# Where k^T v and one subtraction stand in the order of a fused attention and feed-forward kernel

## The chip, the cores and the metric

The kernel runs on one core of a Trainium2 chip. The core has a matrix engine (TensorE, PE in the profile), a vector engine (VectorE, DVE), an activation engine (ScalarE, ACT), a general engine (GpSimd, POOL) and DMA queues; each engine works through its own list of instructions in order, and semaphores hold an instruction back until what it needs is there. The metric is the device time of one execution in microseconds (us). The time before is 917.43 us, the median of three runs (916.87 to 917.55).

## What is computed

Two blocks follow each other. The first is an attention without softmax, with a norm over each head's output; the second a feed-forward block with a squared ReLU:

```python
kv = np.einsum('bhsd,bhse->bhde', k, v)          # 8 x 8 heads, 576 x 64 each
out = np.einsum('bhsd,bhde->bhse', q, kv)
rms = np.sqrt(np.mean(out * out, axis=-1, keepdims=True) + 1e-06)
x = out / rms * g_norm                            # laid out as (4608, 512)
h = x @ w_in                                      # (4608, 2048)
g = s * np.maximum(h, 0.0) ** 2 + b
result = g @ w_out                                # (4608, 512)
```

All data is float32.

## The kernel before

**Units.** The 4608 tokens are cut into 36 chunks of 128, and four chunks make a unit, so there are nine units, u = 0 to 8. In each unit the first product (x times w_in), the activation, and the second product (g times w_out) are done for 512 tokens, both with Strassen-like schemes: sums and differences of quarters are made on DVE, seven products are made on PE instead of eight, and their results are put together again while they are read out of PSUM. Units 2 to 8 use the scheme at two levels in many places. Beside this work, the attention of the next unit is prepared, in two pairs of chunks, A and B.

**The order is written by hand.** No planner moves anything. The first product of units 2 to 8 is `mm1_deep`, whose `run` (line 928) lists the steps one by one: `x1`, `x6`, `y7`, `x5`, `y4` are products of full 128 by 128 tiles, `small(...)` are those of the second level with 128 columns, `a22(s)` reads a y bank. Between them stand calls `at(n)`, and what is done at mark n is given by the table `first` in `sides` (line 1658). In the kernel before, for units 3 to 7, the table has the turn of pair A's q at mark 2, A's product at 4, `back` at 5, the square and B's turn at 6, the row sum and, behind it, k^T v at 7, the norm at 8, B's product at 10, and so on.

**The attention steps.** `product` (line 553) multiplies the turned q with the block-diagonal matrix `bd_kv` in small tiles (64 rows by 32 columns), line 561. `kv_product(b)` (line 370) makes k^T v for one batch with 144 matmuls of 64 by 64 tiles (line 382), and four ACT copies (line 398) put the result into `bd_kv[b % 2]`. The batch is given by `kv_due`: 2 to 7 in units 1 to 6. The k and v rows come through the same ring of buffers in SBUF as the weights of the second product; `used(...)` gives ring slots back in order, and the next loads are issued then.

**PSUM.** Four groups of banks: `ps_t` (tag t, two buffers) for the small products of the attention and for k^T v; `sx` for the second level; and in `ps_f` the x banks (two), the y banks (two) and the z bank (one) for the large products. `bank_of(key, tag, bufs)` takes the next bank of a tag. A bank is used again when its last reader is done.

**The second product.** For units 2 to 8 the function `rest` (line 1377) inside `mm2` lists the steps. Names: a group such as 25 stands for the products 2 and 5 of the outer level. `go_25(m)` issues product m of the inner level on PE; `out_25(m)` reads its result on DVE (line 1092, about 0.35 to 0.5 us); `do_25(m)` is both, one after the other; `sums_25(...)` makes the sums on DVE (lines 250 and 253). `s2` and `s4` are four DVE subtractions each, one for every quarter of the hidden dimension, of 128 by 512 elements:

```python
def s4(steps=range(NS)):
    for s in steps:
        sub(ga["a12", s], ga["a12", s], ga["a11", s])
```

The result of s4 is an operand of the group 73. Around it the order is: `do_25(4)`, `do_6(2, 6)`, then all four s4, `go_6(7)`, `do_6(5)`, the sums of 73, `go_73(1)`, and so on to `do_73(2)`, `sums_73((7,))`, `do_73(6)`, `sums_73((3,))`, `go_73(7)`.

Of the kernel before, what the change touches and what calls it, by code (L numbers as in the profile page):

```python
# [9 lines left out]
FP32 = mybir.dt.float32  # L10
# [6 lines left out]
def kernel(  # L17
# [40 lines left out]
    P = 128  # L58
    B, H, S, D = q.shape
# [23 lines left out]
    ps_t = ctx.enter_context(tc.tile_pool(name="ps_t", bufs=2, space=bass.MemoryType.PSUM))  # L83
# [283 lines left out]
        for _ in range(n):  # L367
            matmul(ps[:, 0, :P], ident, ident, True, True)

    def kv_product(b):  # L370


        ps = [ps_t.tile([P, 2, D], FP32, name="kv_ps", tag="t") for _ in range(2)]
        for i in range(2):
            if b == 0:
                warm((18, 7)[i])
            kv = [kv_in.pop((b, 2 * i + l)) for l in range(2)]
            for j in range(R):
                for l in range(2):
                    for r in range(2):  # L380
                        rows = slice(r * HB, r * HB + HB)
                        nc.tensor.matmul(  # L382
                            ps[r][(r ^ l) * HB : (r ^ l) * HB + HB, i, :],
                            lhsT=kv[l][0][rows, j, :],
                            rhs=kv[l][1][rows, j, :],
                            start=(j == 0),
                            stop=(j == R - 1),
                        )
        for r in range(2):
            rs = slice(r * HB, r * HB + HB)  # L390
            for l in range(2):
                cs = slice((r ^ l) * HB, (r ^ l) * HB + HB)
                to = bd_kv[b % 2][rs, l:NP:2, rs].rearrange("p i (c e) -> p i c e", c=KC)
                src = ps[r][cs].rearrange("p i (e c) -> p i c e", c=KC)
                if b == 0 and l == 1:
                    nc.vector.tensor_copy(out=to, in_=src)
                else:
                    nc.scalar.copy(to, src)
# [248 lines left out]
    def bank_of(key, tag, bufs=2):  # L647
        bank[key] = ps_f.tile([P, 2, TB], FP32, name=f"{tag}_ps", tag=tag, bufs=bufs)
        return bank[key]
# [420 lines left out]
    def mm2(u, step=None, side={}):  # L1070
# [133 lines left out]
        def store(name, j, c, cols=slice(0, DM), queues=(nc.gpsimd, nc.gpsimd)):  # L1204
            view = out_9 if c < R else out_18
            w = view.shape[2]
            for s, (b, jj) in enumerate((b, jj + i) for b, jj, n in parts(c) for i in range(n)):
                queues[s % 2].dma_start(  # L1208
                    out=view[b, jj, :, cols], in_=st[name, j][s * w : s * w + w, cols]
                )  # L1210
# [36 lines left out]
# [3 lines that stand above are left out]
# [127 lines left out]
        def rest():  # L1377
            do_1(1)
            step["x3"]()
            step["x3_square"]()  # L1380
            step["y4"]()
            do_1(2)
            step["y4_square"]()
            do_1(6)
            step["x3_s1"]()
            go_1(7)
            do_1(5)
            sums_25((5, 6), 2)
            sums_25((7,), 5)
            at(0)  # L1390
            do_25(1)
            do_1(3)
            sums_25((5, 6), 5)
            do_1(4)
            do_25(2)
            at(1)
            step["x3_s3"]()
            s2((0,))
            do_25(6)
            s2((1,))  # L1400
            sums_25((3,))
            go_25(7)
            s2((2,))
            do_25(5)
            s2((3,))
            sums_6(())
            do_6(1)
            sums_6((5, 6))
            at(2)
            do_25(3)  # L1410
            sums_6((7, 3))
            do_25(4)
            if end:
                for j in range(2):
                    store("o1", j, 4 * u + j, left, queues)
            do_6(2, 6)
            s4((0, 1))
            s4((2, 3))
            go_6(7)
            do_6(5)  # L1420
            sums_73((5, 6), 7)
            sums_73((), 3)
            go_73(1)
            with_5(0, cols[0])
            out_73(1)
            do_6(3)
            with_5(0, cols[1])
            sums_73((5, 6), 3)
            do_6(4)
            with_5(1)  # L1430
            do_73(2)
            sums_73((7,))
            at(3)
            do_73(6)
            sums_73((3,))
            at("sums")
            go_73(7)
            do_73(5)
            sums_4((5, 6))
            do_4(1)  # L1440
            at(4)
            do_73(3)
            with_7(0)
            sums_4((7, 3))
            go_73(4, 7)
            out_73(4, slice(0, 1))
            with_7(1)
            if end:
                for j in range(2):
                    store("o2", j, 4 * u + 2 + j, right, queues)  # L1450
                store("o1", 0, 4 * u, right, queues)
            else:
                store("o1", 0, 4 * u, queues=queues)
            do_4(2, 6)
            go_4(7)
            do_4(5)
            at(5)
            go_73(4, 3)
            out_73(4, slice(1, 2))
            if end:  # L1460
                store("o1", 1, 4 * u + 1, right, queues)
            else:
                store("o1", 1, 4 * u + 1, queues=queues)
            do_4(3)
            at(6)
            if end:
                store("o2", 0, 4 * u + 2, left, queues)
            else:
                store("o2", 0, 4 * u + 2, queues=queues)
            do_4(4)  # L1470
            if end:
                store("o2", 1, 4 * u + 3, left, queues)
            else:
                store("o2", 1, 4 * u + 3, queues=queues)
# [183 lines left out]
    def sides(u, A, B):  # L1658

        first, second = {}, {}
        kv = []
        if u in kv_due:
            kv.append(lambda: kv_product(kv_due[u]))
            kv.append(lambda: used(*((u, "kv", (n, m)) for n in range(NP) for m in range(2))))
        q = {half: [partial(loads, u + 2, half)] for half in range(2)}
        if u == 1:
            for s in range(1, NS):
                first[((0, 1), (0, 3), (1, 1))[s - 1]] = list(sums_w_in(s))  # L1670
            first.update({
                (1, 3): kv,
                (2, 0): [partial(A["turn"], 0), partial(A["turn"], 1)],
                (2, 1): [A["product"]],
                (2, 2): [A["back"]],
                (2, 3): [A["square"]],
                (3, 0): [A["row_sum"]],
                (3, 2): [A["norm"], A["turn_x"]],
                (3, 3): [lambda: [load() for load in load_q(12, rest_on=nc.sync)]],
            })  # L1680
            return first, second
        if u + 1 == U:
            return first, second
        if u == 2:
            first = {
                4: [A["turn"]],
                5: kv,
                8: [A["product"]],
                9: [A["back"], B["turn"]],
                10: [A["square"]],  # L1690
                11: [A["row_sum"]],
                12: [B["product"]],
                13: [A["norm"]],
                14: [A["turn_x"]],
                15: [B["back"], *q[0]],
                18: [B["square"]],
            }
            second = {
                0: [B["row_sum"]], 1: [A["scale"]], 2: [B["norm"]], 3: [B["turn_x"], *q[1]],
                "sums": [B["scale"]],  # L1700
            }
        else:
            first = {
                2: [A["turn"]],
                4: [A["product"]],
                5: [A["back"]],
                6: [A["square"], B["turn"]],
                7: [A["row_sum"], *kv],
                8: [A["norm"]],
                9: [A["turn_x"]],  # L1710
                10: [B["product"], *q[0]],
                11: [B["back"], A["scale"]],
                12: [B["square"]],
                13: [B["row_sum"]],
                14: [B["norm"]],
                15: [B["turn_x"], *q[1]],
            }
            second = {1: [B["scale"]]}
        second[5], second[6] = [[lambda n=n: x_sums(u + 1)[n]()] for n in range(2)]
        return first, second  # L1720

    for u in range(U):
        A, B = pairs_of(u + 1) if u + 1 < U else (None, None)
# [92 lines left out]
```

## Time and profile before

| | |
|---|---|
| time, median of 3 runs | 917.43 us |
| span of the profiled execution | 915.9 us, 19161 instructions |
| PE (matmul) busy | 903.1 us, 99% |
| DVE busy | 695.5 us, 76% |
| ACT busy | 254.3 us, 28% |
| DMA | 180.33 MB, 197 GB/s on average |
| k^T v matmuls (line 382) | 1152, of which 864 from the ring |
| TensorE clock granted | 0.999 |

In the profile every matmul is two instructions on two tracks: PEld for the load of the weights and PE for the product. A float32 product of the program is two such pairs, so a product with eight matmuls in the profile has four in the program. A line such as "0.48 DVE L1092 ... x1 [0.18 <-PE z_ps L91]" reads: a duration of 0.48 us, the engine, the line of the program, the operands, how many in a row, and that the engine stood idle for 0.18 us before it until PE had written z_ps. PE is shown as busy nearly all the time, so what it loses is found in three ways: in its waits, in what the chain that ended last holds apart from PE, and in the lengths of stretches that hold the same work.

### The profile page before, as it was taken

How to read it: one execution, taken by the hardware profiler on the slowest of the kernel's cores; microseconds unless marked ns; L12 is line 12 of the kernel's file. 1: busy time of each engine (PE TensorE's matmuls, PEld its weight loads, DVE VectorE, ACT ScalarE, POOL GpSimd, SP SyncE). 2: the span in 40 equal slices, each digit the busy share in tenths (PEclk: the TensorE clock that was granted, in tenths of full speed). 3: DMA queues.
4: the chain of work that ended last, by engine and by line, in shares of the span. 5: the costliest groups of instructions: out<-in, count | busy, mean ns of one | idle time of the engine just before them, and what ended most of it. 6: DMA issues, size and time to landing. Idle time of an engine off the chain costs nothing.

```text
span 915.9 us, 19161 instructions
## 1 busy us (share of the span) xinstructions
PE 903.1 (99%) x7524; PEld 827.9 (90%) x7524; DVE 695.5 (76%) x1266; ACT 254.3 (28%) x463; POOL 223.5 (24%) x418
## 2 busy tenths in 40 slices
PE   7999999999999999999999999999999999999998
PEld 7888888888889998999899988999899989999997
DVE  2779778688568986888678867886788778874786
ACT  3774122211135014410343015401450035002500
POOL 2000016114622332801283026503340300020000
PEclk9999999999999999999999999999999999999999
DMA  9677937339943994379436945596538811881185
GB/s 267 214 276 271 267 94 230 96 92 385 340 131 90 290 309 138 84 250 307 145 104 196 293 163 162 131 308 222 150 98 284 281 36 53 278 298 49 54 255 183
DMA packets 120137, 180.33 MB, mean 197 GB/s; under 512 B 29168, under 2 KB 46320, under 8 KB 120048
## 3 DMA queue, kind: packets, MB, share of 16 engines
q1 hardware_dynamic: 101552, 153.00, 53.2%
q0 software_dynamic: 15040, 23.88, 8.6%
q10 hardware_dynamic: 3456, 2.23, 1.0%
q8 instruction: 60, 0.98, 0.4%
q14 instruction: 29, 0.24, 0.1%
HBM read 153.36 MB, written 25.69 MB: 195 GB/s over the span
## 4 chain that ended last, share of the span: by engine, by line
PE 86%; DVE 11%; issue 1%; DMA 1%; ACT 0%; SPq 0%; DVEq 0%
PE x_ps L91 43%; PE y_ps L91 26%; PE z_ps L91 7%; PE sx_ps L91 4%; DVE a L253 2%; PE y_ps L561 2%; DVE sub L253 2%; PE kv_ps L382 2%; DMA kv_sb<-in_v_dram 1%; DVE sub L250 1%; DVE o L1092 1%; DVE b_row L250 1%; DVE r L1092 1%; DVE o L250 1%; DVE w_dn L245 0%
## 5 line engine op out<-in xcount | busy, mean ns | idle before, releaser
L1633 POOL DMA_DIRECT2D q_sb<-in_q_dram x256 | 143.7, 569 | 141.5 <-issue 116.4
L1208 POOL DMA_DIRECT2D out_dram<-o x110 | 54.8, 505 | 408.1 <-DVE o L1092 285.0
L91 PE MATMUL x_ps<-w_sb,sub 128*128 128x128 f32 x1176 | 149.4, 276 | 0.1
L91 PEld LDWEIGHTS x_ps<-w_sb,sub 128*128 128x128 f32 x1176 | 139.7, 192 | 1.2 <-DVE r L1092 0.5
L91 PE MATMUL y_ps<-xs,wb 128*128 128x256 f32 x512 | 121.1, 381 | 0.7 <-DVE ss L584 0.7
L91 PE MATMUL x_ps<-xs,ws 128*128 128x256 f32 x512 | 121.3, 380 | 0.0
L91 PEld LDWEIGHTS y_ps<-xs,wb 128*128 128x128 f32 x512 | 94.6, 190 | 14.6 <-issue 2.8
L91 PEld LDWEIGHTS x_ps<-xs,ws 128*128 128x128 f32 x512 | 93.9, 190 | 11.4 <-issue 0.4
L91 PE MATMUL x_ps<-xT,wa 128*128 128x256 f32 x384 | 89.0, 381 | 0.1
L829 ACT COPY a<-x_ps 128x512 f32<-128x512 f32 x28 | 16.4, 586 | 257.8 <-PE x_ps L91 257.8
L91 PEld LDWEIGHTS x_ps<-xT,wa 128*128 128x128 f32 x384 | 71.3, 190 | 10.9 <-issue 1.3
L250 DVE TENSOR_TENSOR r<-sx_ps,a 128x256 f32<-128x256 f32 x63 | 26.7, 423 | 59.0 <-PE sx_ps L91 58.9
L91 PE MATMUL x_ps<-w_sb,a 128*128 128x128 f32 (+1 forms) x432 | 64.9, 298 | 0.0
L91 PE MATMUL y_ps<-w_sb,a 128*128 128x128 f32 (+1 forms) x416 | 62.1, 295 | 0.0
L91 PEld LDWEIGHTS x_ps<-w_sb,a 128*128 128x128 f32 x432 | 59.0, 191 | 3.3 <-issue 0.4
L91 PEld LDWEIGHTS y_ps<-w_sb,a 128*128 128x128 f32 x416 | 56.1, 192 | 2.1
L1092 DVE SCALAR_TENSOR_TENSOR r<-x_ps,s_col,o 128x256 f32<-128x256 f32 (+1 forms) x84 | 34.7, 413 | 29.1 <-PE x_ps L91 27.8
L91 PE MATMUL y_ps<-w_sb,sub 128*128 128x128 f32 x392 | 50.2, 277 | 2.3 <-DVE sub L253 2.3
L91 PEld LDWEIGHTS y_ps<-w_sb,sub 128*128 128x128 f32 x392 | 46.5, 192 | 3.7 <-DVE sub L253 3.7
L250 DVE TENSOR_TENSOR a<-y_ps,r 128x512 f32<-128x512 f32 x36 | 24.8, 688 | 32.3 <-PE y_ps L91 23.8
L253 DVE TENSOR_TENSOR a<-a,a 128x512 f32<-128x512 f32 x72 | 46.8, 685 | 0.4
L91 PE MATMUL z_ps<-w_sb,a 128*128 128x128 f32 (+1 forms) x352 | 46.8, 280 | 0.0
(190 smaller groups left out, 1489.5 us busy)
## 6 DMA issues: line engine op xcount, KB each, us to landing
w_sb<-w SPq DMA_DIRECT2D x385, 256.0 KB, 4.4
w_raw<-in_moe_w_in_dram SPq DMA_DIRECT2D x8, 1024.0 KB, 7.6
w_raw<-in_moe_w_out_dram SPq DMA_DIRECT2D x8, 1024.0 KB, 5.2
w_sb<-w SPq DMA_DIRECT2D x14, 512.0 KB, 10.2
w<-sub POOLq DMA_DIRECT2D x28, 256.0 KB, 6.3
w_sb<-in_k_dram SPq DMA_DIRECT2D x24, 288.0 KB, 4.6
w_sb<-in_v_dram SPq DMA_DIRECT2D x24, 288.0 KB, 4.7
out_dram<-o POOLq DMA_DIRECT2D x92, 64.0 KB, 3.5
```

The lines of the kernel that those rows point to most:

```text
L91: nc.tensor.matmul(o, lhsT=lhsT, rhs=rhs, start=start, stop=stop, skip_group_check=True)
L250: nc.vector.tensor_tensor(out=o, in0=a, in1=b, op=ALU.add)
L253: nc.vector.tensor_tensor(out=o, in0=a, in1=b, op=ALU.subtract)
L382: nc.tensor.matmul(ps[r][(r ^ l) * HB : (r ^ l) * HB + HB, i, :], lhsT=kv[l][0][rows, j, :], rhs=kv[l][1][rows, j, :], start=(j == 0), sto ...
L561: nc.tensor.matmul(ps[l][32 * p : 32 * p + 32, r, lo:hi], lhsT=bd_kv[b % 2][rows, p, at : at + 32], rhs=st["qT"][rows, p, lo:hi], start=Tr ...
L829: nc.scalar.copy(g_tile("a11", s), st["x", s])
L1092: nc.vector.scalar_tensor_tensor(o, ps, s_col, other, ALU.mult, ALU.add)
L1208: queues[s % 2].dma_start(out=view[b, jj, :, cols], in_=st[name, j][s * w : s * w + w, cols])
L1633: load()
```

## The change

Two things are moved; no work is added or left out.

First, in units 3 to 6, k^T v is no longer done at mark 7 behind A's row sum, but at mark 4, right behind A's product. As the two `ps_t` banks are then still full of that product, k^T v takes the z bank and one y bank instead; `kv_product` has a new argument `beside` for this. Units 0 to 2 keep the old banks and places. The purpose is to let the two kinds of small-tile matmuls follow each other, and to have the ACT copies and the ring's slots earlier.

Second, in `rest`, that is in units 2 to 8, the first of the four s4 subtractions is made before `do_6(2, 6)` and not after it.

```diff
-    def kv_product(b):
-
-
-        ps = [ps_t.tile([P, 2, D], FP32, name="kv_ps", tag="t") for _ in range(2)]
+    def kv_product(b, beside=False):
+        if beside:
+            ps = [
+                bank_of("kv", tag, bufs).rearrange("p b (m d) -> p (b m) d", d=D)[:, :2]
+                for tag, bufs in (("z", 1), ("y", 2))
+            ]
+        else:
+            ps = [ps_t.tile([P, 2, D], FP32, name="kv_ps", tag="t") for _ in range(2)]
...
+            s4((0,))
             do_6(2, 6)
-            s4((0, 1))
-            s4((2, 3))
+            s4((1, 2, 3))
             go_6(7)
             do_6(5)
...
-            kv.append(lambda: kv_product(kv_due[u]))
+            kv.append(lambda: kv_product(kv_due[u], u > 2))
...
             first = {
                 2: [A["turn"]],
-                4: [A["product"]],
+                4: [A["product"], *kv],
                 5: [A["back"]],
                 6: [A["square"], B["turn"]],
-                7: [A["row_sum"], *kv],
+                7: [A["row_sum"]],
```

## The prediction

> **What bounds the kernel now.** I read the page first, then the waits of PE, then the chain of waits in order of time, and last the timeline around the two places that the change touches.
>
> ```profile
> PE 903.1 (99%) x7524; PEld 827.9 (90%) x7524; DVE 695.5 (76%) x1266; ACT 254.3 (28%) x463; POOL 223.5 (24%) x418
> ...
> PE 86%; DVE 11%; issue 1%; DMA 1%; ACT 0%; SPq 0%; DVEq 0%
> ```
>
> PE is the bound. The change removes no work, so it can only give back PE's idle time and the time that PE spends changing from one kind of tile to another. But 11% of the chain that ended last is DVE: there are stretches where PE follows DVE closely. The waits of PE show how little is really lost (columns: total us, times, longest):
>
> ```profile
> PE y_ps L91 <- DVE sub L253: 2.3, 7, 0.5
> ...
> PE y_ps L91 <- DVE ss L584: 0.7, 1, 0.7
> ```
>
> The first is one wait in each of the units 2 to 8. The timeline of unit 3 shows where it comes from (start, duration, engine, in brackets the idle time before):
>
> ```profile
> 409.58 0.48 DVE L1092 SCALAR_TENSOR_TENSOR o<-y_ps,s_col,r 128x256 f32<-128x256 f32 x1
> ...
> 410.24 0.35 DVE L1092 SCALAR_TENSOR_TENSOR o<-z_ps,s_col,r 128x128 f32<-128x128 f32 x1 [0.18 <-PE z_ps L91]
> ...
> 411.13 0.35 DVE L1092 SCALAR_TENSOR_TENSOR r<-x_ps,s_col,o 128x128 f32<-128x128 f32 x1 [0.54 <-PE x_ps L91]
> 411.40 2.49 DVE L253 TENSOR_TENSOR a<-a,a 128x512 f32<-128x512 f32 x4
> ...
> 419.60 1.28 DVE L253 TENSOR_TENSOR sub<-a 128x512 f32<-128x512 f32 x2
> ...
> 420.33 2.05 PE L91 MATMUL y_ps<-w_sb,sub 128*128 128x128 f32 x16 [0.31 <-DVE sub L253]
> ```
>
> The reader is to see: DVE idles twice (0.18 and 0.54 us) while it waits for do_6(2) and do_6(6). Then it gets four s4 subtractions in a row and has no pause until 420.33, where PE stands and waits for the subtraction that go_73(7) uses as its weights.
>
> The second place is the stretch from the attention product of pair A (L561) to y4(0), in units 3 to 7 (the windows table: length, then PE busy and instructions):
>
> ```profile
> 343.33:354.24 10.91, 10.91 (x222) 9.57 (x221) 6.36 (x11) 2.71 (x4) 0.97 (x2) 1.00 0.12 28
> 440.18:451.82 11.64, 10.97 (x221) 9.74 (x221) 6.70 (x11) 3.08 (x6) 0.81 (x2) 1.00 0.15 33
> 537.82:548.73 10.91, 10.91 (x221) 9.56 (x221) 6.36 (x11) 2.71 (x4) 0.89 (x2) 1.00 0.12 28
> 634.73:645.64 10.91, 10.91 (x222) 9.57 (x221) 6.36 (x11) 2.71 (x4) 0.65 (x2) 1.00 0.10 22
> 731.75:740.29 8.54, 8.54 (x77) 7.38 (x77) 4.00 (x8) 2.71 (x4) 1.15 (x3) 1.00 0.25 63
> ```
>
> Units 3 to 6 hold the 144 small k^T v matmuls, unit 7 doesn't. The difference is 2.37 us; unit 4 loses another 0.73 us.
>
> **What the Trainium skill says.** "TensorEngine Tiling (Array Packing)", Key Properties: changing the tiling mode drains the TensorE. The trace agrees. Going back to full tiles, the last small matmul is followed 0.09 us later than the pace, and the first full product lasts 1.99 us where others of its shape last 1.89, because its first weight load is no longer hidden: 0.19 us in all. "Runtime: NRT & Kernel Launch", Instruction fetch mechanics: instructions come in 16 KiB blocks of 256 through the sequencer's own DMA queue. The page agrees: 0.98 MB in 60 packets for about 15,400 PE instructions.
>
> ```profile
> q8 instruction: 60, 0.98, 0.4%
> ```
>
> (That section also calls the fetch hidden by a floor on issue; the k^T v part issues 288 instructions in 2.3 us, so I don't count on it.)
>
> **Part 1: one s4 sooner.** s4((0,)) now stands after out_25(4) (409.58), ahead of out_6(2) and out_6(6); three are left after them. Four of them start to end take 2.49 us and one 0.69, so one costs (2.49 − 0.69)/3 = 0.60 us of DVE. Does it fit? It starts at about 409.98, out_6(2) then starts at 410.58 instead of 410.24 and is followed 0.26 us later (the pace of two such rows in unit 2), at 410.84. out_6(6) isn't ready before 411.13, when PE is done. So the idle time swallows it. Queued behind s4(0) are out_6(2), whose z bank nobody needs soon, and out_6(6), which go_6(5) waits for and which isn't late. Its own inputs are there: s2 is done and the a12 quarter that it overwrites was last read in do_25(1).
>
> So everything from 411.40 on moves up by 0.60 us on DVE, unless it then waits for PE. I went through it: go_6(5), go_73(1), go_6(3), go_6(4) end 0.5 to 1 us or more before DVE wants them; the closest is out_73(2), ready at about 418.27, wanted at 418.60. The weights of go_73(7) then are ready at 419.73 instead of 420.33. PE would reach that load at 419.75: the last matmul before it starts there. What PE loses now is 0.47 us from that matmul to 420.33 beyond its pace of 0.11, and 0.10 on the second matmul, whose weight load isn't hidden (2.05 us for 16 against 1.95). Together 0.57 us. All of it goes, with 0.02 us to spare, and next to none may stay: from 0.4 to 0.57.
>
> The six units 3 to 8 show the same gaps (0.18, 0.54) and the same stall: 6 × 0.57 = 3.4 us. In unit 2 DVE also has norm and turn_x and no idle time there at all: s4(0) delays out_6(6), so go_6(5) starts 0.6 us later, and the later stall is 0.6 us shorter. I count nothing. After go_73(7) DVE waits for PE again (1.74 us idle at 424.21), so the gain isn't lost later. The small stall of 0.17 us at 430.33, where go_4(5) waits for out_4(6), hangs on work behind that point and stays.
>
> **Part 2: k^T v behind the product.** Before, each of units 3 to 6 pays: full to product, product to full, full to kv, kv to full. After: full to product, product to kv, kv to full. What kv costs today beyond its own pace: 2.37 + 0.10 (first y4 load) = 2.47 us; its steady pace in the records is four matmuls per 58.5 ns, 36 × 0.0585 = 2.11. So 0.36 us for in and out, 0.19 of it out, 0.17 in. Removed: 0.19 (product to full) and 0.17 (full to kv). Added: product (64x32 tiles) to kv (64x64 tiles), which the trace doesn't show. Lower end 0, if nothing drains; upper end 0.36, a full change both ways. I take 0.15 to 0.17, like full to kv, since the mode changes all the same. That leaves 0.2 us, four times: 0.8 us (0 to 1.4).
>
> New waits? The two banks: z was last read by the add of small(2,0) at 438.71 in unit 4, the y bank by the last unit; kv would start at 441.27. The next user of z is small(2,0,7). The four bd_kv copies (1.07 us, ACT, behind the x6(0) copy that ends at 440.9) free z by about 444.4; that matmul comes after y7(0) and two small ones, at about 445.9. y7(0) uses the other y bank, free at 435.7. Nothing waits. The loads of k and v: the last is issued at 428.67 and lands in at most 5.0 us (3.8 to 5.0 in this window), 7 us ahead. y4(0) now follows small(2,0) without kv between: it needs a22(0)'s read of y, which ends about 1.1 us before. Behind row_sum, the root no longer has four copies behind it, and the ring's next weights are asked for some 6 us sooner; PE waits for neither, so both are worth nothing.
>
> **Part 3: the 0.7 us of unit 4.** The wait is put down to the sum ss, but y4(0) needs no ss, and in unit 3 it starts before ss ends (354.24 against 354.58). What differs: a fetch of q8 falls in the middle of kv (issued 449.55, landed 450.47; PE goes on at 451.82, 1.35 later). With a fetch due every 256 instructions and 352 in the joined burst, each unit holds at least one. A fetch starts at the earliest 152 instructions past a multiple of 256, and unit 4 stood 193 past the next one. Counting in the new order from the first mark to the second gives 7.8, 10.0, 6.4 and 3.2 us in units 3 to 6, where unit 4 now had 3.7 and stood (an estimate: where the marks lie is read from the records). So unit 4's stall goes (−0.7) and a new one may come in unit 6, 0 to 1 us; I take 0.2. Net −0.5.
>
> **Sum.** −3.4 − 0.8 − 0.5 = −4.7: 917.4 − 4.7 = 912.7 us.
>
> **The rivals.**
> 1. Only part of part 1 arrives: the margin of 0.02 us is missed, 0.1 to 0.2 us stay in each unit, and the joined burst runs into a fetch stall of the size seen (0.7) once or twice. −3.4 + 1 − 0.4 − 0.7 + 1.0 = −2.5: 914.9. For it: the thin margin and unit 6. Against: each wait is short and the DVE chain has 0.3 us or more everywhere else.
> 2. DVE stays the bound: the pull-ahead is lost at another wait on the way, part 1 gives nothing, part 2 and 3 give 1.3 to 1.5: 916.0. Against: I found no such wait between 411.40 and 419.60.
> 3. Slower: the joined burst outruns its instructions in all four units by 0.7 us or more, product to kv costs the full 0.36, and s4(0) only moves the stall to go_6(5), as in unit 2: 4 × 0.7 = 2.8, less unit 4's old 0.7: 919.5. Against: the idle 0.18 and 0.54 us in six of seven units, and three of four counts above are over 6 us.
>
> **How the numbers follow.** Forecast 0.72, rival 1 0.16, rival 2 0.08, rival 3 0.04. Lower end: product to kv free (−0.6 more), no new fetch stall (−0.2), a little of the spread: 911.4. Upper end takes in rival 1: 915.3. Faster by over 0.2% (1.83 us, under 915.6): the forecast and rival 1, 0.88; rival 2 falls within 0.2%, 0.08; slower 0.04.
>
> **What would show it.** Right: "y_ps <- DVE sub L253" falls from 7 waits to one, in unit 2, or none; go_73(7) lasts 1.95 us; the DVE row of s4 after out_6(6) shows x3; the stretch from L561 to y4(0) is about 10.7 us in units 3 to 6 and none has 11.6; the copies to bd_kv start about 3 us after the product. Wrong: a new wait of PE on ACT (bd_kv) at small(2,0,7) or on DVE at go_6(5) in units 3 to 8; a gap after kv without an engine behind it; product to kv over 0.4 us.

## The result, and the profile after

| | before | changed |
|---|---|---|
| time, median (lowest to highest) | 917.49 us (916.87 to 917.63) | 912.25 us (911.96 to 912.49) |
| ratio, with 95% interval | | 0.9944 [0.9927, 0.9961] |
| the same pair, measured again (`after_again`) | 917.33 us | 913.21 us, 0.9956 [0.9943, 0.9968] |
| span of the profiled execution | 915.9 us | 910.7 us |

The change saves 5.2 us in the first pair and 4.1 us in the second; 912.7 us had been predicted. The page of the changed kernel, busy times and the shares of the chain that ended last:

```profile
PE 900.6 (99%) x7524; PEld 827.4 (91%) x7524; DVE 694.3 (76%) x1266; ACT 254.0 (28%) x463; POOL 223.4 (25%) x418
...
PE 95%; DVE 3%; DMA 1%; ACT 0%; issue 0%; ACTq 0%; DVEq 0%
```

The busy times differ little (PE by 2.5 us), since no work went. What changed is the chain: DVE's share of it fell from 11% to 3%. The waits of PE in the changed kernel (total us, times, longest):

```profile
PE xT_ps L496 <- DVE xn L478: 1.5, 1, 1.5
PE warm_ps L91 <- POOL ident masks.py:199: 1.4, 1, 1.4
PE kv_ps L389 <- DMA kv_sb<-in_v_dram: 1.0, 3, 0.5
PE x_ps L91 <- DVE qT L444: 0.8, 1, 0.8
PE x_ps L91 <- DVE r L1099: 0.7, 1, 0.7
PE y_ps L91 <- DVE inv L476: 0.4, 1, 0.4
PE y_ps L91 <- DVE wb L245: 0.3, 1, 0.3
```

Three rows of before are missing: the seven waits on "sub L253", the 0.7 us on "ss L584", and 0.2 us at the start of the program, on "b_sq L357", which the change doesn't touch. One is new: "DVE r L1099", once, 0.7 us. (The lines behind `kv_product` stand seven higher now: 1099 is the read on DVE that was 1092, 568 the attention product, 389 the matmul of k^T v.) The timeline of unit 3 in the changed kernel, around the s4 subtractions:

```profile
409.35 0.68 DVE L253 TENSOR_TENSOR a<-a,a 128x512 f32<-128x512 f32 x1
...
409.95 0.34 DVE L1099 SCALAR_TENSOR_TENSOR o<-z_ps,s_col,r 128x128 f32<-128x128 f32 x1
...
410.50 0.35 DVE L1099 SCALAR_TENSOR_TENSOR r<-x_ps,s_col,o 128x128 f32<-128x128 f32 x1 [0.21 <-PE x_ps L91]
...
410.77 1.89 DVE L253 TENSOR_TENSOR a<-a,a 128x512 f32<-128x512 f32 x3
...
418.37 1.28 DVE L253 TENSOR_TENSOR sub<-a 128x512 f32<-128x512 f32 x2
...
419.24 1.95 PE L91 MATMUL y_ps<-w_sb,sub 128*128 128x128 f32 x16
```

One s4 now fills the idle time ahead of out_6(2) and out_6(6), of which 0.21 us is left, three follow, and go_73(7) at 419.24 has no wait in brackets and lasts 1.95 us. The windows from A's product to y4(0), units 3 to 7 of the changed kernel (length, then PE busy, PEld, DVE, ACT, POOL):

```profile
342.90:353.71 10.81, 10.81 (x221) 9.59 (x221) 3.99 (x8) 3.75 (x8) 0.70 (x2) 1.00 0.67 191
438.98:449.85 10.87, 10.87 (x221) 9.65 (x221) 4.00 (x8) 3.75 (x8) 1.38 (x3) 1.00 0.68 189
535.29:546.10 10.81, 10.81 (x221) 9.59 (x221) 3.99 (x8) 3.75 (x8) 0.99 (x3) 1.00 0.72 208
631.43:642.25 10.82, 10.82 (x222) 9.52 (x221) 4.00 (x8) 3.75 (x8) 1.06 (x3) 1.00 0.73 213
727.68:736.22 8.54, 8.54 (x77) 7.38 (x77) 3.99 (x8) 2.71 (x4) 1.23 (x3) 1.00 0.26 63
```

Where k^T v is done, the stretch has gone from 10.91 to 10.81 us (10.87 in unit 4, whose 11.64 is gone). Unit 7, without k^T v, has its 8.54 us still.

**A measure for single parts.** From one execution to the next, the time up to B's product in unit 2 varies by more than a microsecond with the same code there (267.30 us in `s4_two`, 268.62 in `after_again`). So the traces are compared by distances: from the first matmul of B's attention product in one unit to that in the next, and from the last of these to the start of PE's last matmul. The distance "2 to 3" holds the second product of unit 2 and the k^T v that is done in unit 3; "6 to 7" holds no k^T v of units 3 to 6; "7 to end" holds the second products of units 7 and 8. All are worked out from the records of PE, in us; where nothing was changed they repeat within about 0.1 us:

| kernel | 2 to 3 | 3 to 4 | 4 to 5 | 5 to 6 | 6 to 7 | 7 to end | sum |
|---|---|---|---|---|---|---|---|
| before | 91.62 | 97.48 | 97.01 | 96.91 | 94.55 | 166.22 | 643.79 |
| changed | 91.43 | 96.14 | 96.25 | 96.15 | 93.98 | 165.08 | 639.03 |
| after_again | 91.43 | 96.08 | 96.30 | 96.14 | 93.97 | 165.07 | 638.99 |
| s4_only | 91.72 | 96.27 | 96.44 | 96.34 | 93.97 | 165.07 | 639.81 |
| kv_only | 91.43 | 96.65 | 96.82 | 97.11 | 94.55 | 166.22 | 642.78 |
| kv_mark2 | 91.64 | 96.85 | 97.11 | 96.91 | 94.55 | 166.22 | 643.28 |
| kv_first | 91.42 | 96.65 | 96.81 | 96.88 | 94.54 | 166.22 | 642.52 |
| kv_zy_at7 | 94.68 | 99.86 | 98.63 | 98.53 | 94.54 | 166.20 | 652.44 |
| fewer_warm | 91.63 | 96.85 | 97.02 | 97.20 | 94.55 | 166.22 | 643.47 |
| s4_two | 91.57 | 96.19 | 96.36 | 96.40 | 94.08 | 165.29 | 639.89 |
| with7_later | 91.26 | 95.91 | 96.08 | 96.24 | 93.80 | 164.73 | 638.02 |
| norm_later | 90.49 | 95.91 | 96.08 | 96.32 | 93.80 | 164.73 | 637.33 |
| norm_shift | 90.51 | 95.93 | 96.08 | 95.97 | 93.80 | 164.73 | 637.02 |

By this measure the change is worth 4.8 us in both of its traces against the one of before. The rest lies in the varying start: B's product of unit 2 comes 0.44 us sooner than before in the first trace and 0.63 us later in the second.

### The profile page after: what moved, and what is told of

It reads as the page before. It is cut to its first block, busy times and chain, and to the rows that moved or that the text cites. A ratio compares the mean times of both kernels' runs of the same rounds, so it can differ in the third digit from the quotient of the medians.

```text
span 910.7 us, 19162 instructions
## 1 busy us (share of the span) xinstructions
PE 900.6 (99%) x7524; PEld 827.4 (91%) x7524; DVE 694.3 (76%) x1266; ACT 254.0 (28%) x463; POOL 223.4 (25%) x418
## 4 chain that ended last, share of the span: by engine, by line
PE 95%; DVE 3%; DMA 1%; ACT 0%; issue 0%; ACTq 0%; DVEq 0%
PE x_ps L91 48%; PE y_ps L91 29%; PE z_ps L91 9%; PE sx_ps L91 4%; PE y_ps L568 2%; DMA kv_sb<-in_v_dram 1%; PE kv_ps L389 1%; PE z_ps L389 1%; DVE sub L253 0%; PE y_ps L389 0%; DVE o L1099 0%; DVE a L253 0%; PE qT_ps L557 0%; DVE xn L478 0%; DVE r L1099 0%
## 5 line engine op out<-in xcount | busy, mean ns | idle before, releaser
L1099 DVE SCALAR_TENSOR_TENSOR r<-x_ps,s_col,o 128x256 f32<-128x256 f32 (+1 forms) x84 | 34.7, 414 | 27.3 <-PE x_ps L91 26.0
L253 DVE TENSOR_TENSOR a<-a,a 128x512 f32<-128x512 f32 x72 | 47.4, 684 | 0.4
L91 PEld LDWEIGHTS z_ps<-w_sb,a 128*128 128x128 f32 x352 | 43.9, 192 | 0.8
```

Of the source, the lines that this page charges most:

```text
L91: nc.tensor.matmul(o, lhsT=lhsT, rhs=rhs, start=start, stop=stop, skip_group_check=True)
L253: nc.vector.tensor_tensor(out=o, in0=a, in1=b, op=ALU.subtract)
L1099: nc.vector.scalar_tensor_tensor(o, ps, s_col, other, ALU.mult, ALU.add)
```

## The experiments

**Each half alone.** `s4_only` is the kernel before with nothing but the subtraction moved; `kv_only` is the changed kernel with s4 put back.

```diff
 # s4_only, from before
+            s4((0,))
             do_6(2, 6)
-            s4((0, 1))
-            s4((2, 3))
+            s4((1, 2, 3))
```
```diff
 # kv_only, from the changed kernel
-            s4((0,))
             do_6(2, 6)
-            s4((1, 2, 3))
+            s4((0, 1))
+            s4((2, 3))
```

> The kernel before with s4((0,)) ahead of do_6(2, 6), k^T v left where it was. My theory (idle time of DVE swallows the subtraction, the stall of go_73(7) goes in units 3 to 8, 6 x 0.57 = 3.4 us; in unit 2 the stall only moves to go_6(5)): 3.4 us less than before, about 914.1; the stretch of unit 4 keeps its 11.64 us. Rival (the subtraction brings nothing, all comes from k^T v): no change, 917.5.

> The kernel before with k^T v behind A's product at mark 4 in the z and y banks, s4 left where it was. My theory (0.2 us per unit for the change of tiles that is saved, and unit 4's fetch stall of 0.6 to 0.7 us gone): 1.3 to 1.5 us less, about 916.1; the stretch L561 to y4(0) 10.7 us in units 3, 5, 6 and all seven waits on DVE sub still there. Rival (the two parts help each other): clearly less than 1.3 us here and more than 5.2 us minus the gain of s4 alone in the pair.

`s4_only` took 913.70 us (before beside it 916.86, ratio 0.9963 [0.9950, 0.9975]), `kv_only` 916.26 us (0.9991 [0.9983, 0.9999]). Most of the gain is the one subtraction. In `kv_only` the waits of PE keep the row that the other half removes:

```profile
PE y_ps L91 <- DVE sub L253: 2.3, 7, 0.5
```

In `s4_only` that row is gone, and "7 to end", which holds two s4 and nothing of the other half, is 166.22 − 165.07 = 1.15 us shorter, 0.57 for each. `kv_only` gained less than expected. Its distances "2 to 3", "3 to 4" and "4 to 5" are 0.19, 0.83 and 0.19 shorter than before, but "5 to 6" is 0.20 longer: PE stands for 0.39 us behind k^T v in unit 6, and no engine is named for it. Nor did `s4_only` behave as expected in unit 4, where the order of before is unchanged:

```profile
439.67:450.58 10.91, 10.91 (x222) 9.57 (x221) 6.36 (x11) 2.71 (x4) 1.55 (x4) 1.00 0.12 27
```

The stretch lasts 10.91 us there, where it lasted 11.64 in the kernel before. So that stall doesn't belong to the order of the products alone: PE has the same matmuls in the same order in both kernels, and one trace has the stall and the other doesn't.

**What saves 0.2 us per unit: the neighbour, or the earlier place?** `kv_mark2` has k^T v with the new banks at mark 2, apart from the product; `kv_first` has it directly ahead of the product.

```diff
 # kv_mark2, from kv_only
-                2: [A["turn"]],
-                4: [A["product"], *kv],
+                2: [A["turn"], *kv],
+                4: [A["product"]],
```
```diff
 # kv_first, from kv_only
-                4: [A["product"], *kv],
+                4: [*kv, A["product"]],
```

> As the run with k^T v alone, but at mark 2, between x1(0) and x1(1), so that full products stand on both sides of it. If the saving of 0.2 us per unit comes from small tiles standing next to small tiles, it is gone here: units 3, 5 and 6 cost the same as before, and what is left is unit 4's stall, 0.6 us, if no other fetch falls badly: 916.9. Rival (it comes from the other banks or from being earlier): the 0.2 us per unit stay, 916.1.

> The kernel before with k^T v at mark 4 in the z and y banks, but ahead of A's product and not behind it (s4 as before). Small tiles again stand next to small tiles, in the other order. If the saving is one change to full tiles and back, each unit is 0.2 us shorter than before, as with k^T v behind: the distance from one B product to the next is 96.65 us in unit 3, against 96.85 before. Rival (what counts is that k^T v follows): 96.85.

`kv_mark2` took 917.05 us (1.0004 [0.9996, 1.0012]): "2 to 3" is 91.64 us, that of before, though banks, copies and ring slots come even earlier; the other units too have what before has without a stall. `kv_first` took 916.14 us (one run; before beside it 916.82), and "2 to 3", "3 to 4" and "4 to 5" are those of `kv_only` (in unit 6 it has a small stall, see below). The neighbourhood of the two kinds of small tiles saves the 0.2 us, in either order; the earlier copies and loads give nothing.

**The other banks at the old place.** `kv_zy_at7` takes the z bank and a y bank, but leaves k^T v at mark 7.

```diff
 # kv_zy_at7, from kv_only
-                4: [A["product"], *kv],
+                4: [A["product"]],
...
-                7: [A["row_sum"]],
+                7: [A["row_sum"], *kv],
```

> The kernel before with k^T v left at mark 7, only in the z and y banks instead of the two t banks (s4 as before). There the z bank holds the result of small(2,0,4), which DVE reads 1.5 us after the matmuls (449.89 to 450.3 in the profile before, behind B's turn): my account says that PE waits about 1.4 us for it in each of units 3 to 6, 917 + 5.6 = 922.5, so the banks are free only at the new place. Rival (the banks are as good at the old place): 917.

It took 926.38 us (1.0100 [1.0083, 1.0117]). The row of waits, and the first k^T v matmul of unit 4:

```profile
PE z_ps L389 <- DVE a L250: 5.9, 4, 1.5
```
```profile
453.34 0.27 PE L389 MATMUL z_ps<-w_sb 64*64 64x64 f32 x1 [1.47 <-DVE a L250]
```

At mark 7 the z bank has just been written by a small product, and DVE has to read it first: four waits of 1.5 us in the row, 1.64 us against the pace of PE. So the new banks could be used only together with the move. That much was expected. The time of 922.5 us that I had expected with it was too low by 4 us: PE also stood for 1.34 us inside k^T v in unit 3 and for 1.37 us right behind it in unit 4, without an engine named. By the distances the kernel is 8.65 us longer than before, and 4 × 1.64 + 1.34 + 1.37, less the 0.63 of unit 4's old stall, gives 8.64; what the medians have beyond that lies in the start.

**What the nameless stalls are.** The prediction had put unit 4's stall down to the instruction fetch. If that is so, fewer PE instructions far ahead must move it. `fewer_warm` is the kernel before with 20 of the 25 products of `warm` left out, which stand at the start of the program and whose results nobody reads: 80 PE instructions.

```diff
-                warm((18, 7)[i])
+                warm((3, 2)[i])
```

> The kernel before with 20 of the 25 products left out [...] (warm(3) and warm(2) for warm(18) and warm(7)): this takes 80 PE instructions out ahead of everything else, so the 256-instruction blocks fall 80 instructions later in the program. Fetch theory: unit 4's stretch from L561 to y4(0) falls from 11.64 to about 10.9 us, and unit 6, which then stands to a block as unit 4 did, gets longer by up to 0.7 us. Rival (unit 4's wait is a data wait, on the sum ss as the profile says): unit 4 keeps 11.64 us and unit 6 its 10.91.

It took 918.0 us (one run; before beside it 916.86). Its windows from A's product to y4(0), units 3 to 6:

```profile
343.98:354.89 10.91, 10.91 (x222) 9.57 (x221) 6.37 (x11) 2.72 (x4) 1.97 (x4) 1.00 0.12 29
440.83:451.74 10.91, 10.91 (x222) 9.56 (x221) 6.37 (x11) 2.71 (x4) 0.71 (x2) 1.00 0.09 21
537.84:548.75 10.91, 10.91 (x221) 9.56 (x220) 6.36 (x11) 2.72 (x4) 1.60 (x4) 1.00 0.12 28
634.75:645.95 11.20, 11.10 (x222) 9.57 (x221) 6.65 (x11) 2.71 (x4) 1.49 (x4) 1.00 0.13 31
```

Unit 4's stall is gone and unit 6 has one, of 0.29 us in the window, with the same work in all four. As `s4_only` also lost unit 4's stall, that half alone would prove little; but in every trace with such a stall a block on the instruction queue q8 lands shortly ahead of PE's going on (times worked out from the records of q8, us):

| stall | block landed | PE goes on | later by |
|---|---|---|---|
| before, unit 4 | 450.47 | 451.82 | 1.35 |
| kv_only, unit 6 | 636.28 | 637.54 | 1.26 |
| fewer_warm, unit 6 | 644.47 | 645.81 | 1.34 |
| kv_zy_at7, unit 3 | 355.56 | 356.86 | 1.30 |
| kv_zy_at7, unit 4 | 455.81 | 457.31 | 1.50 |
| with7_later, unit 6 | 634.00 | 635.44 | 1.44 |
| norm_later, unit 6 | 633.64 | 635.13 | 1.49 |
| kv_first, unit 6 | 635.71 | 637.22 | 1.51 |
| s4_two, unit 6 | 634.74 | 636.32 | 1.58 |

The count of PE's instructions settles it. At each of the nine stalls, the number of PE's records (products, weight loads, semaphore waits) that come before the one that goes on late is a multiple of 256 and 193 more: 7617 in before, 5825 and 7617 in `kv_zy_at7`, 11201 in the six others. The instructions themselves differ: one of k^T v in two cases, matmuls or weight loads of the full product behind it in the others. A wait for data has no reason to follow this count; why it is 193, no run shows. And in all thirteen traces no instruction at such a place, 193 past the k-th multiple of 256, starts less than 1.26 us after the k-th block has landed.

In the changed kernel the block in unit 6 landed at 634.53, and the instruction at this place started at 636.02, 1.49 us later: PE lost nothing there. In `s4_only`'s unit 4 the block landed at 449.44, 9.8 us after the stretch begins, where in the kernel before it took 10.3; and with the waits on s4 two semaphore waits of PE are gone ahead of it, so that the place lies two instructions, 0.2 us, later.

**Two s4 subtractions ahead.** Is one the right number?

```diff
 # s4_two, from the changed kernel
-            s4((0,))
+            s4((0, 1))
             do_6(2, 6)
-            s4((1, 2, 3))
+            s4((2, 3))
```

> The changed kernel with two of the four s4 ahead of do_6(2, 6) instead of one. By my account DVE has 0.18 + 0.54 us idle there, room for one subtraction of 0.60 and not for two: out_6(6) comes about 0.5 us late, go_6(5) waits for it 0.4 to 0.5 us in each of units 3 to 8, and the later stall is gone already, so nothing is won: 912.2 + 2.5 to 3 = 915. Rival (sooner is better, DVE has slack there): no slower than 912.2.

It took 913.62 us (0.9963 [0.9948, 0.9978]) where some 915 had been expected. The timeline of unit 3:

```profile
409.22 1.28 DVE L253 TENSOR_TENSOR a<-a,a 128x512 f32<-128x512 f32 x2
...
410.42 0.34 DVE L1099 SCALAR_TENSOR_TENSOR o<-z_ps,s_col,r 128x128 f32<-128x128 f32 x1
...
410.69 0.34 DVE L1099 SCALAR_TENSOR_TENSOR r<-x_ps,s_col,o 128x128 f32<-128x128 f32 x1
...
411.08 1.16 PE L91 MATMUL x_ps<-w_sb,sub 128*128 128x128 f32 x8
```

The read of the x bank starts at 410.69, about 0.3 us after it could, but go_6(5) isn't wanted by PE until some 0.24 us after that read is done in the changed kernel. I had counted the delay and not this slack. What remains is the 0.1 us by which go_6(5) lasts longer (1.16 against 1.06): 0.05 to 0.14 us a unit in most distances; "5 to 6" also holds a fetch stall of 0.14 us. In unit 2 the wait grows from 0.7 to 1.3 us. By the distances one subtraction is better than two by 0.9 us; the intervals of the times overlap.

**Can the rest be had too?** The last four runs were made together on one chip, with `after_again`, the changed kernel as it is, among them. The prediction had left two waits: 0.17 us of go_4(5) on out_4(6) in each unit, and unit 2. `with7_later` makes do_4(2, 6) ahead of with_7(1), a DVE addition whose result PE doesn't wait for:

```diff
+            do_4(2, 6)
             with_7(1)
...
-            do_4(2, 6)
             go_4(7)
```

`norm_later` also takes B's norm and turn_x out of DVE's way in unit 2, and `norm_shift` is that kernel with four warming products fewer, 16 PE instructions, to move where the fetch falls in unit 6:

```diff
 # norm_later, from with7_later
-                0: [B["row_sum"]], 1: [A["scale"]], 2: [B["norm"]], 3: [B["turn_x"], *q[1]],
-                "sums": [B["scale"]],
+                0: [B["row_sum"]], 1: [A["scale"]], "sums": [B["norm"]],
+                4: [B["turn_x"], *q[1], B["scale"]],
```
```diff
 # norm_shift, from norm_later
-                warm((18, 7)[i])
+                warm((16, 5)[i])
```

> The changed kernel again, beside the other three on one chip, so that the sum of the parts can be compared with the whole. The parts alone gave -3.2 us (s4) and -0.6 (k^T v), the whole -5.2 at first. My theory (the parts add up, and the difference of about 1.4 us is fetch stalls and the start, which fall differently in each execution): 3.8 to 5.2 us less than before. Rival (the two parts help each other): again 5.2 or more, and stalls in the parts alone that the whole hasn't.

> The changed kernel with the addition with_7(1) (0.42 us on DVE) moved behind out_4(6), and the stores with it. The wait of go_4(5) for out_4(6), 0.17 us in each of units 2 to 8, should go: 7 x 0.17 = 1.2 us less than the changed kernel. Rival (the wait comes back at the next reader, go_4(3) or the next unit's first product): no gain.

> As with_7(1) later, and in unit 2 B's norm goes from mark 2 to the mark sums and B's turn_x and scale to mark 4, out of the stretch in which DVE has no idle time. Unit 2 then should look like units 3 to 8: the 0.93 us at go_6(5), the 0.1 at go_73(7) and the 0.33 at go_73(5) go, 1.0 to 1.3 us more than with_7(1) alone. Rival (the norm takes DVE's 1.7 us of idle time before out_73(5) and PE then waits at go_4 or in the next unit): half of it or nothing.

> As the run with the norm later, and 4 of the 25 warming products at the start left out (warm(16), warm(5)), which moves the 256-instruction blocks by 16: in unit 6 the block that follows k^T v is then needed 16 instructions, about 1.7 us, later, so the stall there that shows in some executions can't come. Fetch theory: the same or up to 0.4 us less, and no gap in unit 6 behind k^T v. Rival (those gaps have another cause): a gap in unit 6 as often as before.

| kernel | time, us | ratio to before, 95% interval |
|---|---|---|
| after_again | 913.21 (912.46 to 914.41) | 0.9956 [0.9943, 0.9968] |
| with7_later | 911.38 (910.97 to 911.80) | 0.9935 [0.9922, 0.9947] |
| norm_later | 911.25 (911.05 to 912.28) | 0.9935 [0.9923, 0.9948] |
| norm_shift | 910.67 (910.34 to 911.37) | 0.9928 [0.9915, 0.9942] |

`after_again` took 4.1 us less than before, within the 3.8 to 5.2 us expected if the parts add up. The distances say the same: `s4_only` has 3.98 us less than before and `kv_only` 1.01; with unit 4's stall of 0.63 us counted once and `kv_only`'s 0.39 us in unit 6 left out, that is 4.75 us, against 4.80 for the whole. Only in unit 6 may one part have helped the other: with four of PE's waits on s4 gone, the place at 193 lies four instructions later in the changed kernel than in `kv_only`, two matmuls or 0.4 us.

`with7_later` has 0.17 us less in "2 to 3", "3 to 4" and "6 to 7" than `after_again`, and 0.34 less in the last, which holds two units. In its timeline of unit 3 the two DVE rows have changed places and PE's product stands without a wait, with its first weight load hidden (1.06 us, where before had 1.16):

```profile
428.10 0.35 DVE L1099 SCALAR_TENSOR_TENSOR r<-x_ps,s_col,o 128x128 f32<-128x128 f32 x1
...
428.37 0.42 DVE L250 TENSOR_TENSOR o<-o 128x256 f32<-128x256 f32 x1
...
428.79 1.06 PE L91 MATMUL x_ps<-w_sb,sub 128*128 128x128 f32 x8
```

In unit 6 it had a fetch stall instead: 0.16 us at 635.44 and 0.10 us of a weight load that isn't hidden behind it. The distances sum to 0.97 us less than `after_again`, and to 1.2 us, as expected, without that stall; the traced executions differ by 2.1 us, of which 1.2 lie in the start. `norm_later` took 0.77 us out of unit 2 ("2 to 3": 90.49 against 91.26) where 1.0 to 1.3 had been expected, because a new gap of 0.38 us came at go_4(5) of that unit; its median moved by 0.1 us only, which can't be told from none. `norm_shift` did to unit 6 what it was made for: no stall, "5 to 6" 95.97 against 96.32. Its median is the lowest of all, 910.67 us; part of that may be the four products fewer, which the distances don't hold. The intervals of these three overlap, so their order among themselves is shown by the traces, not by the times. All three medians lie below that of the changed kernel beside them.

## Why the prediction was right, step by step

**Part 1, one s4 sooner: right in mechanism and size.** Predicted 6 × 0.57 = 3.4 us. Matmul by matmul, each of units 3 to 8 loses a gap of 0.47 us and the 0.10 us of an unhidden weight load, together 3.43 us; `s4_only` shows it without the other half. The thin margin of 0.02 us held in each of these units, so rival 1, in which part of the stall stays, didn't come. Unit 2 was counted at nothing, and the trace of the changed kernel shows why, at the place that the prediction named:

```profile
314.13 0.34 DVE L1099 SCALAR_TENSOR_TENSOR r<-x_ps,s_col,o 128x128 f32<-128x128 f32 x1
...
314.52 1.16 PE L91 MATMUL x_ps<-w_sb,sub 128*128 128x128 f32 x8 [0.67 <-DVE r L1099]
```

PE waits 0.59 us more here than before and 0.60 less at go_73(7). Where DVE has no idle time, the move only carries the stall to another place. Rival 2, DVE as the bound all along, is that picture in all seven units; it held in this one.

**Part 2, k^T v behind the product: right in mechanism and in the net size; two entries of its sum were too large and cancelled.** Predicted 0.2 us a unit; measured 0.20, 0.19 and 0.19 in units 3, 5 and 6: 0.10 us in the stretch and 0.10 of y4's first weight load behind it. To get there the prediction took away 0.17 us for the change from full tiles to k^T v, and added 0.15 to 0.17 for the change from product to k^T v. By the starts of the matmuls both are 0.09 us. In before, k^T v starts 0.205 us behind the last full matmul, where the pace is 0.112. The product's last matmul is followed after 0.306 us by full tiles in before and after the same 0.306 us by k^T v in the changed kernel; the prediction reckoned the former as 0.09 us later than the pace, so the latter is that too. A change between the two kinds of small tiles thus comes as late as one to full tiles, and what is saved is one change (0.09) and one weight load that wasn't hidden after the return to full tiles (0.10). That the 0.2 came out although both entries were nearly twice too large is luck: they cancel. The Trainium skill says that changing the tiling mode drains the TensorE ("TensorEngine Tiling (Array Packing)", Key Properties); the 0.09 us at each of these changes agrees, and so do the 0.2 us between `kv_mark2` and `kv_first`. No wait of PE on the bd_kv copies came; they start at 346.30 in unit 3, 3.4 us after the start of the product.

**Part 3, unit 4's stall: right about the new order, wrong in taking the old stall for sure.** Eight traces have k^T v beside the product. None has a stall in units 3, 4 or 5; five have one in unit 6, of 0.14 to 0.39 us, which is the unit that the prediction had counted as the tightest. The two of the changed kernel have none, so the 0.2 us booked for unit 6 weren't needed there, and the net is 0.63 us instead of 0.5. But the step booked −0.7 as if the kernel before always had that stall. `s4_only` lost it with the old order of the products, and no run shows how often the executions behind the median of before have it. The term belongs in the range and not in the sum. The Trainium skill calls the cost of crossing a block "mostly hidden" ("Runtime: NRT & Kernel Launch", Instruction fetch mechanics). For most of the blocks the traces agree: in the changed kernel every block but that of unit 6 lands over 2.6 us before PE starts the instruction at its place. In and right behind bursts of small tiles they don't, with up to 1.4 us in `kv_zy_at7`.

**The sum.** 3.43 + 3 × 0.19 + 0.77 (unit 4: 0.63 and its part of the neighbourhood) = 4.8 us, against 4.7 predicted; that is also what the distances give. Rival 3, slower by stalls in all four units, saw the right mechanism: in `kv_zy_at7` two of four units have it. With k^T v beside the product, the traces show at most one, in unit 6, of 0.4 us or less.

## What to carry to other kernels

A wait of PE that stands at a matmul may be paid for far ahead: follow the waiting engine back to its last idle time, and move there a piece of its work whose inputs are ready and which nobody queued behind it needs soon. Then check in each unit that this idle time exists, since in the one without it the stall only changed its place. Put small-tile products of different shapes next to each other, so that the array goes to full tiles and back once. And where PE stands in or behind a dense burst and no engine that it needs is late, look for an instruction block that has just landed: here the place of such stalls followed the number of instructions ahead, and their cost was a chance, not a term.

## What the hardware showed that was not expected

- PE goes on 1.26 to 1.58 us after an instruction block has landed, in all nine stalls seen, and always at an instruction that stands 193 past a multiple of 256. So the places can be counted ahead of a run; whether the block is late there differs from trace to trace.
- A change of tile shape delayed the next matmul by 0.09 us against the pace before it, from full tiles to 64x64 (0.205 us against 0.112), from 64x32 back to full tiles, and as much from 64x32 to 64x64 (0.306 us both). Going back to full tiles cost 0.10 us more, for a weight load that isn't hidden.
- With the same number of PE instructions ahead, unit 6 has no such stall in the two traces of the changed kernel and one of 0.14 to 0.30 us in `s4_two`, `with7_later` and `norm_later`. One trace shows that a stall can come at a place and not that it does.
- Sixteen PE instructions fewer at the start of the program went with 0.35 us less in unit 6, some 600 us later ("5 to 6": 96.32 to 95.97, once each).
